# Linear attention with a gated MLP on one core: other positions for the opening, all-VectorE gates and w_in conversions, and x split anew

## The chip, the core and the metric

One core of a Trainium2 chip runs the whole program as one launch. The metric is the device time of an execution in microseconds. A core has TensorE (PE), VectorE (DVE), ScalarE (ACT) and GpSimd (POOL), and SyncE (SP), whose queue here issues all transfers. Each engine works through its own row of instructions in order, and semaphores make one wait for another.

## The reference

An attention with a state of 40x40 for each of 4 batches and 8 heads runs over 768 positions, and its output, 4 x 768 x 320, goes through a gated MLP. Cut to what matters:

```python
for t in range(S):                                   # attention, r k v w a b: (4, 8, 768, 40)
    y[:, :, t] = einsum('bhd,bhde->bhe', rt, state)
    Sa = einsum('bhde,bhe->bhd', state, at)
    state = state * wt[:, :, None, :] - einsum('bhd,bhe->bhde', Sa, bt) \
            + einsum('bhd,bhe->bhde', vt, kt)
x = y.transpose(0, 2, 1, 3).reshape(B, S, H * D)
h = x @ w_in                                         # w_in: (320, 1024)
h = 0.5 * h * (1.0 + tanh(c * (h + 0.044715 * h ** 3)))
u, v = h[..., :512], h[..., 512:]
v_n = (v - mean(v)) / sqrt(var(v) + 1e-06) * g_ln
v_s = einsum('ts,bsd->btd', w_sg, v_n) + b_sg[None, :, None]
return x + (u * v_s) @ w_out                         # w_sg: (768, 768), w_out: (512, 320)
```

## The kernel before

**Attention.** The 768 positions are cut into 12 chunks c of 64, and the 32 heads of all batches into two half-batches f of two batches each. Inside a chunk the recurrence is a triangular system, and between chunks a state `sc` of 40x40 per head is carried.

- *Gates* (`gate_1` to `gate_n`): for each (c, f), VectorE multiplies up the decays (`ex` by scans), makes `at`, and then twice reciprocal, scan (`fixed`) and product: `kb`. TensorE multiplies `ab` from at and kb (16 x 2 products for each half of kb), and transposes kb into `kt`. ACT copies `kbt<-kt` and writes ab's strictly lower blocks as `nts`; VectorE masks what is left of ab back into the tile `at`. `n` is nts transposed by 32x32 blocks.
- *Substitution* (`inv_load`, `inv_in`, `inv_sub`, `inv_end`, `inv_turn`): POOL inverts the triangular blocks of a group of chunks by 29 steps of two operations, `tg<-x,n` and `x<-x,tg`. The groups are (0), (1), (2, 3), (4, 5), (6, 7), (8, 9), (10, 11). VectorE writes n ahead of it and finishes x behind it, then transposes it: `x1z`, `xt`.
- *Back step and chain*: `gp`, `gs`, `xp` turn the inverses into `xt` of a chunk (`post_x`). Then `ru`, `rhsb`, `us`, `vu`, `ut`, `vut`, `pq`, `sp`, `yp` and `yt` follow for each f, and yt goes to `xd`, a copy of x in DRAM.

**MLP.** All products run on a pair of numbers, a high part (h) and a low part (l), both of a short type, in three matmuls. `split64` makes such parts of a stored weight in six steps: the load, ACT's scaled field, VectorE's integer `fields`, ACT's rounding (`wvh`, `wuh`), and `low`, three subtractions on VectorE or POOL. Parts of the MLP run beside the attention as soon as 128 positions of a batch are in xd: `fill_x`, `fill_split`, `fill_low`, `fill_v` and `fill_out` make five of six tiles of v for each batch (`hf`, `hv`), and keep hv in `hd` in DRAM. Here the split halves `xfh` and `xfl` of x go to `xhd` and `xld` in DRAM, too, and `split_x` reads them back in the dense part. For batch 0, `in_v` turns a tile v (two `p` steps on ACT, v on VectorE, then `vh` on ACT and `vl` on POOL) while the last chunk runs. What is left for the end is the dense part: `sg` (w_sg, as `wsh` and `wsl`, by the parts of v), `hf` for u, `gx`, and the output products `op`.

**Order.** No scheduler decides. Each step is registered with a position, and `in_order` sorts all of them; then they are written into the program in that order, so that two steps on one engine stand as their positions do:

```python
y, n = YG[c], GATE[f]
at_(y + n[0], gate_1, c, f, 0)
...
z, v = YI[GROUPS.index(g)], INV if len(g) > 1 else INV1
at_(z + v[0], inv_load, g)
```

`YG` places the gates, `YC` the chains and back steps, `YI` the groups, `DEC` the weight conversions with the steps of `DSTEP` and `DSTEPF` (the first four), `PF` the in_v of batch 0, `BLANKS` POOL's memsets. All engines' calls go through one wrapper, `InOrder.call`, so that every row of the profile has its line, L179; steps are told apart by their tiles.

Of the kernel before, what the change touches and what calls it, by code (L numbers as in the profile page):

```python
# [37 lines left out]
WARMS = ((-4.831, 8), (-4.331, 8))  # L38
BLANKS = -21.0
ZEROS = -36.0  # L40
LOADS = -24.0
# [16 lines left out]
INV1 = (-44.0, -29.3, -27.1, 0.429, -2.0, -1.3)  # L58
BACK = (-3.831, -0.954, -1.454, -2.595, -0.449, 1.071, 3.249)
END_GT = 232.184  # L60
END_IW = 279.907
END_RING = 292.105
END_IV = 314.249
# [25 lines left out]
PO = 232.204  # L89
DECO = (277.194, 283.194, 289.194, 295.194, 301.194, 307.194, 313.194, 319.194)  # L90
# [595 lines left out]
class Mlp:  # L686
# [3 lines left out]
    def __init__(self, tc, ps, xd, w_in, w2, g_ln, wst, b_sg, w_out, decays, out):  # L690
# [6 lines left out]
        self.sb, self.done, self.hd, self.xhd, self.xld = None, set(), None, None, None  # L697
# [176 lines left out]
    def split_cols(self, t, h, l):  # L874
        self.A.copy(out=h, in_=t)
        self.V.tensor_tensor(out=l, in0=t[:, 0:2], in1=h[:, 0:2].bitcast(F32), op=ALU.subtract)
        self.V.tensor_tensor(out=h[64:128, 2], in0=t[64:128, 2], in1=h[64:128, 2].bitcast(F32), op=ALU.subtract)

    def split_x(self, b, n):
        e = 128 * LASTF  # L880
        if (b, 0) not in self.done:
            c = slice(384 * n, 384 * n + 384)
        elif n == 0:
            self.Q.dma_start(out=self.xh[:, :, 0:e].bitcast(F32), in_=self.xhd[b, :, :, 0:e])
            self.Q.dma_start(out=self.xl[:, :, 0:e].bitcast(F32), in_=self.xld[b, :, :, 0:e])
            return
        else:
            c = slice(e, S)
        self.split_cols(self.xts[b % 2][:, :, c], self.xh[:, :, c], self.xl[:, :, c])
# [151 lines left out]
    def side(self):  # L1041
# [38 lines left out]
        for k, p in enumerate(PF):  # L1080
# [5 lines left out]
    def run(self, ahead, verdict=None):  # L1086
# [18 lines left out]
        names = [*FIRSTS] if ahead else [*FILLERS, *FIRSTS]  # L1105
# [75 lines left out]
def attention_then_gated_mlp(tc, ins, out):  # L1181
    nc = tc.nc
    a = ins
    with ExitStack() as ctx:
# [74 lines left out]
```

## Time and profile before

| | |
|---|---|
| time, median of 3 runs | 695.72 us (695.24 to 705.01) |
| the profiled execution | 702.58 us |
| its span, first to last instruction | 700.5 us |
| busy: PE, PEld, DVE, ACT, POOL | 558.7, 509.5, 486.9, 336.1, 351.9 us |
| mean granted TensorE clock | 0.864 of full speed |

The rows below are of the profiled execution, with times from the start of its span. An engine's busy share is a mean over an opening, twelve chunks and a dense part with different limits, so that rows are read by stretch.

### The profile page before, as it was taken

What the parts mean: (1) busy time and instruction counts of PE and PEld (TensorE: products, weight loads), DVE (VectorE), ACT (ScalarE), POOL (GpSimd) and SP (SyncE); (2) the same over time, 40 slices, a digit from 0 to 9 for tenths busy, and PEclk for the clock granted to TensorE, in tenths of its full rate; (3) what the DMA queues carried; (4) which work ended last, traced back from release to release, by engine and by line L of the source; (5) the groups of instructions that cost most, each with busy time, mean ns of one, the idle gap of its engine ahead of it and who ended that gap; (6) DMA issues with size and microseconds to landing.
All of it is one profiled execution on the core that took longest, in us unless ns stands there. A gap on an engine that the chain in (4) does not pass through costs nothing.

```text
span 700.5 us, 25303 instructions
## 1 busy us (share of the span) xinstructions
PE 558.7 (80%) x10710; PEld 509.5 (73%) x10710; DVE 486.9 (70%) x950; ACT 336.1 (48%) x736; POOL 351.9 (50%) x596
## 2 busy tenths in 40 slices
PE   4452766835989989798986979679779999899996
PEld 4352765724878878677875768469779998799995
DVE  5673677766656867765868756537568889969942
ACT  3330547424565767566675566625334434434510
POOL 3186842945585487177566843323244333334331
PEclk8556666765789999899998899779899999999999
DMA  5460262333256565765555556655601465232001
GB/s 185 119 167 6 80 151 83 103 92 106 80 152 163 150 173 149 200 155 138 155 149 153 140 159 167 181 176 159 219 30 63 145 222 153 89 132 73 29 23 39
DMA packets 87138, 89.50 MB, mean 128 GB/s; under 512 B 38280, under 2 KB 69000, under 8 KB 85000
## 3 DMA queue, kind: packets, MB, share of 16 engines
q1 hardware_dynamic: 87016, 87.79, 44.3%
q8 instruction: 86, 1.41, 0.9%
q14 instruction: 36, 0.29, 0.1%
HBM read 68.10 MB, written 19.66 MB: 125 GB/s over the span
## 4 chain that ended last, share of the span: by engine, by line
PE 44%; DVE 16%; issue 6%; ACT 4%; POOL 2%; DMA 2%; SPq 1%; POOLq 0%; ACTq 0%; DVEq 0%
PE sg L179 10%; PE hf L179 5%; PE yp L179 5%; PE op L179 3%; PE ru L179 3%; DVE v L179 3%; PE ut L179 3%; PE pq L179 3%; PE sp L179 2%; DVE p L179 2%; PE ab L179 2%; DVE cv L179 2%; PE xp L179 2%; DVE g L179 2%; PE kt L179 2%
## 5 line engine op out<-in xcount | busy, mean ns | idle before, releaser
L179 POOL TENSOR_TENSOR tg<-x,n 128x135 f32<-128x135 f32 (+25 forms) x203 | 104.1, 513 | 79.9 <-issue 30.7
L179 POOL TENSOR_TENSOR x<-x,tg 128x135 f32<-128x135 f32 (+25 forms) x203 | 106.1, 523 | 15.8
L179 PE MATMUL ab<-at,kb 64*64 64x64 f32 x1536 | 42.4, 268 | 56.3 <-DVE fixed L179 22.7
L179 PEld LDWEIGHTS ab<-at,kb 64*64 64x64 f32 x1536 | 36.9, 175 | 61.0 <-issue 31.8
L179 ACT ACTIVATE nts<-ab 32x512 f32<-32x512 f32 x96 | 46.3, 483 | 57.3 <-PE ab L179 54.4
L179 PE MATMUL sg<-wsh,vh 128*128 128x384 f32 x192 | 66.7, 347 | 5.8 <-ACT wsh L179 3.4
L179 PE MATMUL sg<-wsl,vh 128*128 128x384 f32 x192 | 67.1, 350 | 4.0 <-POOL wsl L179 2.9
L179 POOL TENSOR_TENSOR gx<-g,gy 128x384 fp32r<-128x384 f32 x32 | 34.0, 1066 | 71.6 <-ACT gy L179 71.6
L179 PE MATMUL sg<-wsh,vl 128*128 128x384 f32 x192 | 66.7, 347 | 0.9 <-POOL vl L179 0.9
L179 DVE TENSOR_TENSOR at<-ab,mask 64x512 f32<-64x512 f32 x48 | 32.2, 678 | 42.9 <-ACT nts L179 32.7
L179 POOL TENSOR_TENSOR rs<-rs,mhalf 128x1 f32<-128x1 f32 x24 | 14.9, 624 | 76.0 <-DVE rs L179 72.4
L179 ACT CAST gy<-g 128x384 fp32r<-128x384 f32 x32 | 16.4, 514 | 62.2 <-DVE g L179 59.4
L179 PEld LDWEIGHTS sg<-wsh,vh 128*128 128x128 f32 x192 | 37.2, 194 | 7.0 <-ACT wsh L179 4.4
L179 ACT CAST vh<-v 128x512 fp32r<-128x512 f32 x24 | 14.6, 619 | 56.4 <-DVE v L179 56.4
L179 PEld LDWEIGHTS sg<-wsl,vh 128*128 128x128 f32 x192 | 37.1, 193 | 5.8 <-POOL wsl L179 3.5
L179 DVE TENSOR_TENSOR pqs<-pq,mask 128x512 f32<-128x512 f32 x48 | 30.7, 681 | 14.5 <-PE pq L179 14.5
L179 DVE TENSOR_TENSOR yt<-yp,ex 128x256 f32<-128x256 f32 x48 | 18.1, 417 | 31.5 <-PE yp L179 30.2
L179 PEld LDWEIGHTS sg<-wsh,vl 128*128 128x128 f32 x192 | 37.3, 194 | 2.1 <-POOL vl L179 2.0
L179 PE MATMUL kt<-ident,kb 128*128 128x128 f32 x192 | 35.2, 342 | 2.8 <-issue 2.8
L179 PE MATMUL ut<-ident,vu 64*64 64x64 f32 x768 | 32.2, 235 | 6.1 <-ACT vu L179 6.1
L179 PEld LDWEIGHTS ut<-ident,vu 64*64 64x64 f32 x768 | 28.1, 146 | 11.3 <-ACT vu L179 8.7
L179 POOL TENSOR_TENSOR vl<-v,vh 128x512 fp32r<-128x512 f32 x24 | 31.6, 1320 | 8.8 <-ACT vh L179 8.8
(154 smaller groups left out, 1554.8 us busy)
## 6 DMA issues: line engine op xcount, KB each, us to landing
main<-main SPq DMA_DIRECT2D x44, 321.4 KB
hd<-hv SPq DMA_DIRECT2D x20, 256.0 KB
v<-hd SPq DMA_DIRECT2D x20, 256.0 KB
vu<-vs SPq DMA_DIRECT2D x24, 160.0 KB
vs<-vb SPq DMA_DIRECT2D x24, 160.0 KB
rt<-rt SPq DMA_DIRECT2D x48, 80.0 KB
vut<-vt SPq DMA_DIRECT2D x48, 80.0 KB
xd<-yt SPq DMA_DIRECT2D x96, 40.0 KB
```

What stands on the lines that cost most here:

```text
L179: return self.tc.keep_in_program_order(f(*a, **k))
```

## The change

1. The first eight gates (chunks 0 to 3) have their own positions, `GATE0`, 9.2 apart, and all their steps are VectorE's (`GATEE` is empty; before, both kb of the first two gates and one at were POOL's). With these positions the kt transposes of a gate stand ahead of its ab on TensorE.
2. Groups 0, 1 and 2 of the substitution have their own positions, `INV0`; chunks 2 to 11 all stand 5.17 earlier on the scale, and with them all that is placed beside them. POOL's memsets go to its start.
3. The low parts of all six w_in conversions are VectorE's; before, those of every second were POOL's. The positions of the six change, and the first four loads are asked for earlier.
4. `xhd` and `xld` are gone: fills store their halves no more, and `split_x` splits x again for both halves of every batch, the cast on ACT, the rest on POOL (before, VectorE, and for the last 128 positions alone).
5. The in_v of batch 0 stand 5 to 9 later against chunk 11, and split_x of its second half stands behind them.

```diff
+GATE0 = {(0, 0): (-50.0, (0, 0.6, 1.2, 2.0, 2.1, 3.5, 5.0, 6.2, 6.1, 10.6, 7.4)), (0, 1): (-40.8, (0, 0.6, 1.2, 2.0,
...
-YI = (-3.831, 23.669, 81.0, 132.0, 183.0, 234.0, 285.0)
-GATEE = {(0, 0): "VG", (0, 1): "GG"}
+GATEE = {}
...
-INV1 = (-44.0, -29.3, -27.1, 0.429, -2.0, -1.3)
+INV0 = {0: (-38.7, -31.7, -29.5, 0.443, -3.5, -2.8), 1: (-9.4, -2.4, -0.2, 0.443, 25.8, 26.5), 2: (19.9, 26.9, 29.1,
+    0.702, 70.1, 70.8)}
...
-DSTEPF = (-2.5, -0.5, 0.0, 0.7, 1.4, 2.4)
-DEC = (5.0, 15.0, 25.0, 35.0, 45.0, 55.0, 241.194, 247.194, 253.194, 259.194, 265.194, 271.194)
+DSTEPF = (-9.0, -0.5, 0.0, 0.7, 1.4, 2.4)
+DEC = (10.0, 22.0, 34.0, 46.0, 58.0, 70.0, 236.025, 242.025, 248.025, 254.025, 260.025, 266.025)
...
-PXS = 314.459
+PXS = 321.28
...
-PF = (303.0, 308.0, 313.0, 318.0, 323.0)
+PF = (302.831, 308.831, 314.831, 320.831, 326.831)
...
-                y, n = YG[c], GATE[f]
+                y, n = GATE0.get((c, f)) or (YG[c], GATE[f])
...
-            z, v = YI[GROUPS.index(g)], INV if len(g) > 1 else INV1
+            z, v = (0, INV0[g[0]]) if g[0] in INV0 else (YC[g[0]], INV)
...
+    def split_x(self, b, n):
+        c = slice(384 * n, 384 * n + 384)
+        t, h, l = self.xts[b % 2][:, :, c], self.xh[:, :, c], self.xl[:, :, c]
         self.A.copy(out=h, in_=t)
-        self.V.tensor_tensor(out=l, in0=t[:, 0:2], in1=h[:, 0:2].bitcast(F32), op=ALU.subtract)
...
-        elif n == 0:
-            self.Q.dma_start(out=self.xh[:, :, 0:e].bitcast(F32), in_=self.xhd[b, :, :, 0:e])
-            self.Q.dma_start(out=self.xl[:, :, 0:e].bitcast(F32), in_=self.xld[b, :, :, 0:e])
...
+        self.G.tensor_tensor(out=h[64:128, 2], in0=t[64:128, 2], in1=h[64:128, 2].bitcast(F32), op=ALU.subtract)
+        self.G.tensor_tensor(out=l, in0=t[:, 0:2], in1=h[:, 0:2].bitcast(F32), op=ALU.subtract)
...
-        self.Q.dma_start(out=self.xhd[b, :, :, c], in_=h.bitcast(F32))
-        self.Q.dma_start(out=self.xld[b, :, :, c], in_=l.bitcast(F32))
...
-                steps[k] = self.split64(*self.weights_in()[k], HF // 2, self.G if k % 2 and k < 6 else self.V)
+                steps[k] = self.split64(*self.weights_in()[k], HF // 2, self.V)
```

How the new positions move instructions is seen in the rows of three engines. The first place is VectorE in the opening. Before, from the first kb of gate (1, 0) to n of group 0 (main and ex are numbered by tile, ab by bank; gate (1, 0)'s are `main_96`, `ab_332` and `ab_333`):

```order
L179 TENSOR_TENSOR kb<-main_96,fixed_95 128x2x4x64
L179 RECIPROCAL fixed_94<-call 128x4
L179 SCALAR_TENSOR_TENSOR fixed_95<-main_96,fixed_94 128x260
L179 TENSOR_TENSOR kb<-main_96,fixed_95 128x2x4x64
L179 SCALAR_TENSOR_TENSOR ex_131<-main_97,fixed_94 128x260 x2
L179 TENSOR_TENSOR at_140<-ab_332,mask 64x8x64
L179 TENSOR_TENSOR at_140<-ab_333,mask 64x8x64
L179 TENSOR_SCALAR call<-ex_131 128x8
L179 TENSOR_TENSOR at_141<-main_97,ex_131 128x8x64
L179 STREAM_TRANSPOSE n<-nts_103 128x32x32
```

After, from the second kb of gate (0, 0), `kb<-main_94`, to n of group 0:

```order
L185 TENSOR_TENSOR kb<-main_94,fixed_93 128x2x4x64
L185 SCALAR_TENSOR_TENSOR ex_127<-main_95,fixed_92 128x260 x2
L185 TENSOR_SCALAR call<-ex_127 128x8
L185 TENSOR_TENSOR at_137<-main_95,ex_127 128x8x64
L185 TENSOR_TENSOR at_136<-ab_218,mask 64x8x64
L185 TENSOR_TENSOR at_136<-ab_219,mask 64x8x64
L185 RECIPROCAL fixed_92<-call 128x4
L185 SCALAR_TENSOR_TENSOR fixed_93<-main_95,fixed_92 128x260
L185 TENSOR_TENSOR kb<-main_95,fixed_93 128x2x4x64
L185 RECIPROCAL fixed_92<-call 128x4
L185 SCALAR_TENSOR_TENSOR fixed_93<-main_95,fixed_92 128x260
L185 TENSOR_TENSOR kb<-main_95,fixed_93 128x2x4x64
L185 STREAM_TRANSPOSE n<-nts_101 128x32x32
```

The masks of a gate now stand behind the next gate's at and ahead of its kb, and n of group 0 stands one gate earlier, behind gate (0, 1)'s kb. What the fence can't show is TensorE's row, which before is ab, ab, kt, kt for each gate and now kt, kt, ab, ab.

The second place is POOL in group 2's substitution, at the second conversion inside it (`stg` and `wvl` are a w_in conversion's low part). Before:

```order
L179 TENSOR_TENSOR x<-x,tg 128x17x15
L179 TENSOR_TENSOR tg<-x,n 128x252
L179 TENSOR_TENSOR x<-x,tg 128x18x14
L179 TENSOR_TENSOR stg_1958<-stg_1958,stg_1952 128x256
L179 TENSOR_TENSOR stg_1937<-stg_1937,wvh 128x256
L179 TENSOR_TENSOR wvl<-stg_1937,stg_1958 128x256
L179 TENSOR_TENSOR tg<-x,n 128x247
L179 TENSOR_TENSOR x<-x,tg 128x19x13
L179 TENSOR_TENSOR tg<-x,n 128x240
L179 TENSOR_TENSOR x<-x,tg 128x20x12
```

After, from the same substitution step on:

```order
L185 TENSOR_TENSOR tg<-x,n 128x255
L185 TENSOR_TENSOR x<-x,tg 128x17x15
L185 TENSOR_TENSOR tg<-x,n 128x252
L185 TENSOR_TENSOR x<-x,tg 128x18x14
L185 TENSOR_TENSOR tg<-x,n 128x247
L185 TENSOR_TENSOR x<-x,tg 128x19x13
L185 TENSOR_TENSOR tg<-x,n 128x240
L185 TENSOR_TENSOR x<-x,tg 128x20x12
```

The three operations of the conversion are gone from POOL's row; they stand on VectorE, the last ones around group 2's closing x steps.

The third place is ACT in the last chunk (`p`, `p`, `vh` are a round of in_v; `xt<-xp` and `rhsb` belong to the chain). Before, for the first half-batch:

```order
L179 CAST xfh<-xf 128x384
L179 ACTIVATE p<-v 128x512
L179 ACTIVATE p<-p 128x512
L179 CAST vh<-v 128x512
L179 COPY xt_99<-xp 32x16x32 x2
L179 ACTIVATE cv<-cv 128x64
L179 CAST woh<-stg 128x64
L179 COPY s_7863<-tp 104x320
L179 COPY s_7868<-tp 104x320
L179 ACTIVATE vu_126<-us_7870 64x4x40 x2
```

After:

```order
L185 CAST xfh<-xf 128x384
L185 COPY xt_97<-xp 32x16x32 x2
L185 ACTIVATE p<-v 128x512
L185 ACTIVATE p<-p 128x512
L185 ACTIVATE cv<-cv 128x64
L185 CAST woh<-stg 128x64
L185 COPY s_7798<-tp 104x320
```

The vh of the round that stood ahead of `xt<-xp` is gone from there, and the next round begins behind it. For the second half-batch, before:

```order
L179 ACTIVATE p<-v 128x512
L179 ACTIVATE p<-p 128x512
L179 CAST vh<-v 128x512
L179 COPY rhsb_117<-ru 128x320
L179 ACTIVATE vu_127<-us_8032 64x4x40 x2
L179 ACTIVATE vu_127<-us_8033 64x4x40 x2
L179 CAST xfh<-xf 128x384
L179 COPY vut_125<-ut 104x8x64
```

After, where `xh<-xt` is the cast of split_x:

```order
L185 COPY rhsb_115<-ru 128x320
L185 ACTIVATE vu_125<-us_7954 64x4x40 x2
L185 ACTIVATE vu_125<-us_7955 64x4x40 x2
L185 CAST xfh<-xf 128x384
L185 ACTIVATE p<-v 128x512
L185 ACTIVATE p<-p 128x512
L185 CAST vh<-v 128x512
L185 CAST xh<-xt_7788 128x3x384
L185 COPY vut_123<-ut 104x8x64
```

The round that stood ahead of rhsb now stands behind vu, together with the cast, both ahead of the second `vut<-ut`.

## Rows read from the trace of the kernel before

**Rows 1.** Windows of all engines: stretch, busy PE, PEld, DVE, ACT, POOL, PEclk, DMA, GB/s.

```profile
113.10:169.40 56.30, 32.81 (x860) 28.93 (x856) 37.31 (x79) 24.55 (x57) 39.53 (x64) 0.69 0.42 109
18.00:30.00 12.00, 6.86 (x139) 5.88 (x140) 8.15 (x15) 3.70 (x8) 1.77 (x2) 0.50 0.28 67
```

**Rows 2.** The same window, conversions' stg tiles alone: busy DVE, ACT, POOL.

```profile
113.10:169.40 56.30, 7.06 (x18) 3.56 (x9) 4.85 (x6) 0.69 0.42 109
```

**Rows 3.** Timeline of group 2: start, us, engine, operation, in brackets idle before.

```profile
110.83 2.16 DVE L179 STREAM_TRANSPOSE n<-nts 128x1024 f32<-128x1024 f32 x1
...
121.72 0.73 POOL L179 TENSOR_TENSOR stg<-stg,stg 128x256 f32<-128x256 f32 x1 [4.06 <-ACT wvh L179]
...
152.20 0.72 POOL L179 TENSOR_TENSOR stg<-stg,stg 128x256 f32<-128x256 f32 x1 [8.14 <-ACT wvh L179]
...
169.35 0.76 DVE L179 SCALAR_TENSOR_TENSOR x<-x,n 128x30 f32<-128x30 f32 x3 [3.85 <-POOL x L179]
```

**Rows 4.** Timeline of the first ex, and of gate (1, 0) to group 0's n.

```profile
6.07 1.28 DVE L179 TENSOR_TENSOR_SCAN ex<-main,fixed 128x260 f32<-128x260 f32 x2 [1.81 <-DMA main<-first]
...
25.09 0.17 DVE L179 RECIPROCAL fixed<-call 128x4 f32<-128x4 f32 x1
...
27.69 0.69 DVE L179 TENSOR_TENSOR kb<-main,fixed 128x512 f32<-128x512 f32 x1
...
28.43 1.14 PE L179 MATMUL ab<-at,kb 64*64 64x64 f32 x32 [0.33 <-DVE kb L179]
...
29.50 1.97 PE L179 MATMUL kt<-ident,kb 128*128 128x128 f32 x8
...
29.60 1.98 ACT L179 ACTIVATE nts<-ab 32x512 f32<-32x512 f32 x4 [3.78 <-PE ab L179]
...
31.61 0.68 DVE L179 TENSOR_TENSOR at<-ab,mask 64x512 f32<-64x512 f32 x1 [0.32 <-ACT nts L179]
...
32.89 2.07 DVE L179 STREAM_TRANSPOSE n<-nts 128x1024 f32<-128x1024 f32 x1
```

**Rows 5.** Timeline, VectorE's closing x step of group 0.

```profile
64.50 0.69 DVE L179 SCALAR_TENSOR_TENSOR x<-x,n 128x15 f32<-128x15 f32 x3 [11.00 <-POOL x L179]
```

**Rows 6.** Groups of the six w_in conversions (idle before at the end), and one on the timeline.

```profile
L179 DVE TENSOR_SCALAR stg<-stg 128x256 f32<-128x256 f32 x6 | 1.8, 302 | 13.5 <-ACT stg L179 13.5
L179 ACT ACTIVATE stg<-stg 128x256 f32<-128x256 f32 x6 | 2.6, 434 | 16.6 <-DMA stg<-w 14.5 <-DMA stg<-w_in 2.1
...
149.98 0.62 DVE L179 TENSOR_SCALAR stg<-stg 128x256 f32<-128x256 f32 x2 [6.25 <-ACT stg L179]
```

**Rows 7.** Timeline, one size of substitution step twice on POOL.

```profile
127.47 0.55 POOL L179 TENSOR_TENSOR tg<-x,n 128x207 f32<-128x207 f32 x1
...
160.64 1.13 POOL L179 TENSOR_TENSOR tg<-x,n 128x207 f32<-128x207 f32 x1
```

**Rows 8.** Timeline of chunk 11, ACT and the two us of TensorE.

```profile
439.86 0.26 ACT L179 ACTIVATE cv<-stg 128x64 f32<-128x64 f32 x1 [3.50 <-DMA stg<-w_out]
...
440.87 0.63 ACT L179 ACTIVATE p<-v 128x512 f32<-128x512 f32 x1
...
444.04 0.62 ACT L179 CAST vh<-v 128x512 fp32r<-128x512 f32 x1 [2.02 <-DVE v L179]
...
445.19 0.43 PE L179 MATMUL us<-rhsb,xt 64*64 64x40 f32 x2 [5.84 <-ACT xt L179]
...
458.36 1.09 PE L179 MATMUL us<-rhsb,xt 64*64 64x40 f32 x32 [3.80 <-ACT rhsb L179]
```

**Rows 9.** Groups on POOL, the fills' low parts: busy, mean ns, idle before.

```profile
L179 POOL TENSOR_TENSOR xfl<-xf,xfh 128x256 fp32r<-128x256 f32 x20 | 15.2, 758 | 41.3 <-ACT xfh L179 30.2 <-PE pq L179 7.5 <-DMA hd<-hv 3.3
L179 POOL TENSOR_TENSOR xfh<-xf,xfh 64x128 fp32r<-64x128 f32 x20 | 9.3, 466 | 1.6
```

**Rows 10.** Timeline early in the dense part.

```profile
504.08 0.51 ACT L179 CAST xh<-xt 128x384 fp32r<-128x384 f32 x1 [5.49 <-DMA xt<-xd]
...
514.51 0.44 PE L179 MATMUL sg<-wsl,vh 128*128 128x384 f32 x1 [1.53 <-POOL wsl L179]
```

More of the change, by code (lines that the diff above doesn't have):

```diff
@@ L37 @@
 WARM = 14
[L38 to L41, printed above, removed]
+WARMS = ((-2.6, 8), (-2.1, 8))
+BLANKS = -55.0
+ZEROS = -35.0
+LOADS = -12.0
 PER = 25.5
@@ L49 @@
     29.01, 31.005))
-YC = (0, 27.5, 81.0, 106.5, 132.0, 157.5, 183.0, 208.5, 234.0, 259.5, 285.0, 310.5)
-YG = (35.908, 55.908, 81.0, 106.5, 132.0, 157.5, 183.0, 208.5, 234.0, 259.5, 285.0, 310.5)
-YI = (-3.831, 23.669, 81.0, 132.0, 183.0, 234.0, 285.0)
-GATEE = {(0, 0): "VG", (0, 1): "GG"}
+YC = (2.231, 31.531, 75.831, 101.331, 126.831, 152.331, 177.831, 203.331, 228.831, 254.331, 279.831, 305.331)
+YG = (45.508, 65.508, 85.508, 105.508, 126.831, 152.331, 177.831, 203.331, 228.831, 254.331, 279.831, 305.331)
+GATEE = {}
 GROUPS = ((0,), (1,), (2, 3), (4, 5), (6, 7), (8, 9), (10, 11))
@@ L57 @@
 INV = (-61.011, -53.011, -50.811, 0.759, -6.51, -5.143)
-INV1 = (-44.0, -29.3, -27.1, 0.429, -2.0, -1.3)
+INV0 = {0: (-38.7, -31.7, -29.5, 0.443, -3.5, -2.8), 1: (-9.4, -2.4, -0.2, 0.443, 25.8, 26.5), 2: (19.9, 26.9, 29.1,
+    0.702, 70.1, 70.8)}
 BACK = (-3.831, -0.954, -1.454, -2.595, -0.449, 1.071, 3.249)
[L60 to L63, printed above, removed]
+END_GT = 227.015
+END_IW = 274.738
+END_RING = 286.936
+END_IV = 309.08
 CG = 0.7978845608028654
 G1 = 0.044715
-PIN = 232.194
+PIN = 227.025
 DSTEP = ((-8.5, -1.0, 0.0, 0.7, 1.4, 2.4), (-8.5, -1.0, 0.0, 0.7, 1.4, 2.4))
-DSTEPF = (-2.5, -0.5, 0.0, 0.7, 1.4, 2.4)
-DEC = (5.0, 15.0, 25.0, 35.0, 45.0, 55.0, 241.194, 247.194, 253.194, 259.194, 265.194, 271.194)
+DSTEPF = (-9.0, -0.5, 0.0, 0.7, 1.4, 2.4)
+DEC = (10.0, 22.0, 34.0, 46.0, 58.0, 70.0, 236.025, 242.025, 248.025, 254.025, 260.025, 266.025)
 GE = "VV"
@@ L73 @@
 LASTF = 5
-PX = 314.449
-PXS = 314.459
-PV = 292.205
-PS = 338.954
-PL = 331.954
-PF = (303.0, 308.0, 313.0, 318.0, 323.0)
+PX = 309.28
+PXS = 321.28
+PV = 287.036
+PS = 333.785
+PL = 326.785
+PF = (302.831, 308.831, 314.831, 320.831, 326.831)
 PH = 9
 FILLERS = ("v0", "v1", "v2", "v3", "v4")
-FIRSTS = ("u1", "u0", "u2", "u3", "v5", "u4", "u5", "u6", "u7")
+FIRSTS = ("u1", "u0", "v0", "v1", "u2", "v2", "u3", "v3", "v4", "v5", "u4", "u5", "u6", "u7")
 SEQ = ("s1", "s2", "s0", "s3", "s4", "v0", "s5", "v1", "o0", "o1", "o2", "s6", "s7", "v2", "u0", "v3", "u1", "v4",
@@ L88 @@
 SGS = (5, 3, 5, 6, 7, 8, 8, 11, 10, 11, 12, 11)
-PO = 232.204
-DECO = (277.194, 283.194, 289.194, 295.194, 301.194, 307.194, 313.194, 319.194)
+PO = 227.035
+DECO = (272.025, 278.025, 284.025, 290.025, 296.025, 302.025, 308.025, 314.025)
 DSTEPO = (-8.5, -1.0, 0.0, 0.7, 1.4, 2.4)
@@ L696, in __init__ @@
         self.vn, self.us, self.gs, self.xf = {}, {}, {}, {}
-        self.sb, self.done, self.hd, self.xhd, self.xld = None, set(), None, None, None
+        self.sb, self.done, self.hd = None, set(), None
         self.n, self.todo, self.plan = 0, [], None
@@ L872, in load_x @@
             Q.dma_start(out=t[64 * k:64 * k + 64, 2, c], in_=self.xd[b, 256:320, c])
-    def split_cols(self, t, h, l):
+    def split_x(self, b, n):
+        c = slice(384 * n, 384 * n + 384)
+        t, h, l = self.xts[b % 2][:, :, c], self.xh[:, :, c], self.xl[:, :, c]
         self.A.copy(out=h, in_=t)
-        self.V.tensor_tensor(out=l, in0=t[:, 0:2], in1=h[:, 0:2].bitcast(F32), op=ALU.subtract)
[L877 to L882, printed above, removed]
-        elif n == 0:
-            self.Q.dma_start(out=self.xh[:, :, 0:e].bitcast(F32), in_=self.xhd[b, :, :, 0:e])
-            self.Q.dma_start(out=self.xl[:, :, 0:e].bitcast(F32), in_=self.xld[b, :, :, 0:e])
[L886 to L889, printed above, removed]
+        self.G.tensor_tensor(out=h[64:128, 2], in0=t[64:128, 2], in1=h[64:128, 2].bitcast(F32), op=ALU.subtract)
+        self.G.tensor_tensor(out=l, in0=t[:, 0:2], in1=h[:, 0:2].bitcast(F32), op=ALU.subtract)
     def fill_x(self, b, k):
@@ L909, in fill_low @@
         E.tensor_tensor(out=h[64:128, 2], in0=t[64:128, 2], in1=h[64:128, 2].bitcast(F32), op=ALU.subtract)
-        c = slice(128 * k, 128 * k + 128)
-        self.Q.dma_start(out=self.xhd[b, :, :, c], in_=h.bitcast(F32))
-        self.Q.dma_start(out=self.xld[b, :, :, c], in_=l.bitcast(F32))
         self.xf[b, k] = h, l
@@ L1079, in side @@
         at(PS, self.split_x, 0, 1)
-        for k, p in enumerate(PF):
+        for k, p in enumerate(PF[:LASTF]):
             at(p - PH, self.load_h, 0, k)
@@ L1104, in run @@
         self.open_rest()
-        names = [*FIRSTS] if ahead else [*FILLERS, *FIRSTS]
+        names = [x for x in FIRSTS if x not in FILLERS[:LASTF]] if ahead else [*FILLERS, *FIRSTS]
         seq, jobs = [(x, 0) for x in names], [] if ahead else [(XS, lambda: self.split_x(0, 1))]
@@ L1192, in attention_then_gated_mlp @@
         part.hd = dr.tile([B, LASTF, 128, HF], F32, name="hd")
-        part.xhd = dr.tile([B, 128, 3, S], F32, name="xhd")
-        part.xld = dr.tile([B, 128, 2, S], F32, name="xld")
         verdict = attention(tc, a, xd, flag, keep, ps, part)
```

5 rows, old and new, of the table GATE0 are left out of this document.

## The prediction

> **What bounds the kernel now.** I read the slices of the page first. POOL and VectorE are busy by turns at the start, and TensorE fills up only from about 175 us on. So there are three regimes, an opening, a steady middle and a dense tail, and each needs its own view. The change writes other positions for the opening alone and for the last chunk, and shifts everything between by one constant; in the middle the order of every engine stays as it was.
>
> In the opening the table by stretch shows what is late. From the start of group 2's substitution to its last step, 113.1 to 169.4, POOL works 39.5 of 56.3 us, VectorE 37.3, TensorE 32.8 [rows 1]. No engine is full, so the timeline is next: POOL stands still twice in that stretch, 4.06 and 8.14 us, both times in front of the low part of a w_in conversion that waits for ACT's cast [rows 3]. The substitution's own steps queue behind it, and VectorE's closing x step then waits for POOL (3.85 us). The conversions' six POOL operations take another 4.85 us there [rows 2]. Thus 56.3 − 12.2 − 4.9 = 39.1 us are substitution itself.
>
> Before that, a gate is a loop of kb on VectorE, ab on TensorE, nts on ACT and a mask on VectorE. From 18 to 30 us TensorE's granted clock is 0.50 of full speed, the 1.2 GHz level, and VectorE is busy 8.15 of 12 us [rows 1]: the loop is latency.
>
> At the end of the attention, chunk 11, TensorE's us waits 5.84 us for ACT's xt and, for the other half-batch, 3.80 us for rhsb [rows 8]. In both cases ACT had a round of a v tile's p, p and vh ahead of it.
>
> **Part by part. First gates.** The first two gates leave POOL: their kb took POOL operations, now all is VectorE's. Before, n of group 0 started at 32.89, behind gate (1,0)'s masks. After, it stands right behind gate (0,1)'s kb. The first ex starts at 6.07, the recip–scan–kb pair ends about 5.3 later at 11.4 (a pair takes 25.09 to 28.38, 3.3 us [rows 4]). Then comes the price of the new order on TensorE: the eight kt run ahead of ab. From a pair's end to its last mask it was 28.38 to 32.29, 3.9 us, since ab of the first kb had run under the pair. Now it is kt 1.97 + twice ab 1.14 + nts 1.98 + mask 0.68 + hand-offs = 7.1 [rows 4]. So gate (0,1)'s pair ends at 11.4 + 7.1 + 3.3 = 21.8, and its nts 6.2 later: n starts at 28.0, 4.9 earlier. Each later gate among the first eight costs 7.1 + 3.3 = 10.4 in place of about 7.9, +2.6 at this clock.
>
> **Groups 0 and 1.** Group 0 took 29.5 us from n's end (34.96 [rows 4]) to VectorE's x at 64.50 [rows 5], and POOL's blanking fills leave its inside: it ends at 59.6 or before. But n of group 1 has, by the new order, gates and a conversion in front on VectorE, at +2.6 a gate: I get 64.4 against 65.2, where x ended. The gain of group 0 is eaten. From there to n of group 2 I walked VectorE's new order row by row with these durations: 42.4 in place of 45.6, thus 106.8 in place of 110.83 [rows 3], with 4 us either way for half of the 2.6 of the three gates between (102.8 to 110.8).
>
> **Group 2.** Its conversions leave POOL: stalls gone, 39.1 us left. VectorE gets them. Of 18 conversion operations in the stretch at 7.06/18 = 0.39 us [rows 2] the order makes 26: 10.2 us. So 37.3 − 7.1 + 10.2 = 40.4. Then come VectorE's waits for ACT, since a conversion goes from ACT's scaled field to VectorE and back: 13.5 us over all six, 6.25 of them at 149.98 [rows 6]. ACT itself waited 16.6 for the loads there [rows 6], and a load now stands 9 in place of 2.5 ahead, so I count 2 to 5 in this stretch and take 44 in all: VectorE takes POOL's place as the bound. Closing x step: 106.8 + 2.2 (n) + 44 = 153.0 against 169.35, 16 earlier. Three conversion operations now stand between x and x1z and three more ahead of the next masks and n: 6 × 0.39 = 2.3, say −3 with a hand-off. **Opening: 13 us, ends 6 and 20**; the unchanged middle carries that on, since there every chunk starts from the one before it.
>
> A row speaks against moving work to VectorE: while POOL substitutes, the same tg of 207 elements takes 0.55 us at 127.47 and 1.13 at 160.64 [rows 7]. *By the rule:* the Trainium skill, GPSIMD Engine Reference, section 8 Key points, says that GpSimd shares its SBUF interfaces with VectorE, with contention when VectorE runs an instruction in a 2-port perf mode or with two SBUF inputs, which the two lengths of that row agree with. Nine added two-input operations, at half a microsecond each, would then lengthen POOL's 39.1 to some 43.6, still under VectorE's 44, so that the sum stands.
>
> **Stores of split halves.** The two stores per fill are gone. SP issues every transfer in order, and these two had to wait there for ACT's and POOL's halves. What that cost others I see in one place, POOL's xfl, 3.3 us behind the hd store [rows 9]. **+1, ends 0 and 3.**
>
> **Chunk 11.** The p rounds go behind xt and rhsb. The first wait, 5.84, keeps the part that comes from cv's DMA (3.50 before 439.86 [rows 8]); the round's own time, 440.87 to 444.66 with VectorE's v in it, is 3.8 and goes. Of the second, 3.80, nearly all goes. Added: one round and an xh cast of three times the old columns (3 × 0.51 = 1.5 [rows 10]) now stand ahead of the second vut, 5.3 us, of which TensorE can fill perhaps half with a fill's matmuls. 3.8 + 3.6 − 2.6 = 4.8, **+5, ends 0 and 7**. At the ends the vut side eats both, or is wholly hidden.
>
> **Dense tail.** x is split anew for each half of each batch. ACT casts 1152 columns for each half, where one cast of 384 did for a batch. POOL gets xl and xh: at the fills' rate per element 3 × 0.758 + 3 × 0.466 = 3.7 us per half [rows 9], 29 us over eight halves, where two loads and two short VectorE steps did before. For later batches ten or so microseconds of TensorE's work lie over each. For the first, the split competes with wsl, which POOL also makes and TensorE already waits for (1.53 us at 514.51), and with the cast that waited 5.49 for the load of x at 504.08 [rows 10]. **−2, ends −5 and 0.**
>
> Sum: 13 + 1 + 5 − 2 = 17. The profiled execution took 702.58 (span 700.5 and 2.08 around it): 685.6. It lies 6.86 above the median of the runs, 695.72, and nothing in the sum depends on that offset: 695.7 − 17 = **679**. All good ends together give 20 + 3 + 7 − 0 = 30, thus 666; all bad ones 6 + 0 + 0 − 5 = 1, thus 695. A measurement of this kernel tells about 2%, 13.9 us, from no change.
>
> **The rivals.** *POOL stays the bound of group 2*, since VectorE's gates hide in the waits for ACT: then n of group 2 starts at 105.3 (1.5 before my value, as its row too has such waits), POOL 39.1 behind its 2.2, x at 146.6, 23 earlier than before, less the 3. The opening gives 20 and the time is about 671. For it speaks that VectorE stood still 19 us of the stretch [rows 1]; against it, that these stillnesses are waits for ACT's nts in the gates, which kt ahead of ab makes longer.
>
> *The gates eat it.* If eight gates each cost 2.6 more and all of that is on the path to n of group 2, that is 21 us against the 12.2 + 4.9 freed on POOL and the 4.9 won at n of group 0: a gain of about 1 in the opening, and with the other terms 3 to 5 in all: 690 to 693. For it: the clock of 0.50 and VectorE waiting for nts. Against: gates of chunks 2 and 3 overlap substitution that was the later one, and the clock in the stretch of group 2 is 0.69 [rows 1].
>
> *Loads that hold VectorE, the slower side.* Six conversions stand in VectorE's in-order row, each with a first step that waits for ACT's scaled field, which waits for its load. One such wait was 6.25 us, at 149.98; behind it now stand group 2's last x, x1z and the next gates. At 3.4 us per conversion ((17 + 3.5 counted)/6) the gain is gone, at 5.7 ((17 + 13.9 + 3.5)/6) the kernel is 2% slower, and at 6.25 for all, 37.5 less 3.5, the time is 713. For it: POOL, which could take such a wait before, no longer does. Against: the six waits sum to 13.5, so 2.25 each, and the earlier load shortens them.
>
> *It doesn't do what it says:* the p rounds behind xt leave v late, the dense tail starts as late as before: without chunk 11's 5 us the time is 684, inside the range.
>
> **How the numbers follow.** The forecast (VectorE bounds group 2, 672 to 688) gets 0.52; POOL as the bound (about 671) 0.15; gates eat it (690 to 694) 0.22; the loads 0.08, its whole chance counted as slower, with what else could go wrong; 0.03 for something better than all. The range 666 to 694 holds the first three with little left out on either side. Faster by over 2% is a time under 681.8: some 0.31 of the forecast's 0.52, all of the 0.15 and the 0.03, thus 0.49; slower 0.08; within 2% the rest, 0.43.
>
> **What would show it.** Right: no POOL wait for wvh inside group 2; its x on VectorE at about 153 and waiting little for POOL; n of group 0 near 28; the first gp of chunk 2 some 13 earlier, and the same lead still there at chunk 10; us of chunk 11 without 5.84 and 3.80. Wrong in size: n of group 2 after 111 or the lead gone by the middle, which would mean another thing than the opening sets the pace there, a load or the dense fills. Wrong in sign: stg rows on VectorE with waits of 2 us and more for ACT, between the last tg and x1z above all. In the tail, xl on POOL ahead of the first wsl, with TensorE's wait at that wsl grown from 1.53 to 5.

## The result and the profile after

The changed kernel took 675.82 us (median of 4 runs, 667.34 to 679.25) against 696.64 for the kernel before in the same rounds; the ratio of the undisturbed runs is 0.9597, with a 95% interval of 0.9478 to 0.9716. Two of the four runs lie over 1.5% above the fastest and are left out of the ratio, which therefore stands for 28 us where the medians are 20.8 apart. In a second set of rounds the kernel took 673.53 (6 runs) against 700.92: 0.9587 (0.9530 to 0.9644). The forecast was 679, faster. Its profiled execution took 673.29 us with a span of 671.3.

First the table by stretch of the changed kernel: group 2's substitution from n's end to the closing x, all engines, and then the conversions' stg tiles alone (VectorE, ACT, POOL).

```profile
102.05:147.95 45.90, 31.95 (x880) 29.01 (x884) 42.06 (x89) 24.75 (x56) 34.43 (x58) 0.76 0.45 110
...
102.05:147.95 45.90, 11.80 (x26) 4.04 (x10) 0.00 (x0) 0.76 0.45 110
```

The stretch is 45.9 us for 56.3 [rows 1]. POOL has no conversion in it and works 34.4 us; VectorE is busy 42.1 of 45.9, 26 conversion steps at 0.45 us among it. POOL's last step, in the next fence, ends at 141.08, 6.8 us ahead of the closing x, which waits for nothing: VectorE has become the bound.

The timeline of the changed kernel: VectorE's n of groups 0 to 2, x of groups 0 and 2, POOL's last step of group 2, the transpose behind x, and TensorE's first gp of chunk 2.

```profile
25.18 2.09 DVE L185 STREAM_TRANSPOSE n<-nts 128x1024 f32<-128x1024 f32 x1 [5.20 <-ACT nts L185]
...
54.51 0.68 DVE L185 SCALAR_TENSOR_TENSOR x<-x,n 128x15 f32<-128x15 f32 x3 [2.51 <-POOL x L185]
...
58.63 2.11 DVE L185 STREAM_TRANSPOSE n<-nts 128x1024 f32<-128x1024 f32 x1
...
99.95 2.10 DVE L185 STREAM_TRANSPOSE n<-nts 128x1024 f32<-128x1024 f32 x1
...
140.64 0.44 POOL L185 TENSOR_TENSOR x<-x,tg 128x87 f32<-128x87 f32 x1
...
147.91 0.76 DVE L185 SCALAR_TENSOR_TENSOR x<-x,n 128x30 f32<-128x30 f32 x3
...
149.44 1.94 DVE L185 STREAM_TRANSPOSE x1z<-x 128x1024 f32<-128x1024 f32 x1
...
151.53 1.92 PE L185 MATMUL gp<-x1z,nts 64*32 64x32 f32 x64 [0.98 <-DVE x1z L185]
```

Against [rows 3 to 5], n of group 0 is 7.7 earlier, n of group 2 10.9, its x 21.4; x does not wait for POOL any more (3.85 before). The first gp of chunk 2 stood at 172.19 in the kernel before, so the opening gives 20.7 us:

```profile
172.19 0.45 PE L179 MATMUL gp<-x1z,nts 64*32 64x32 f32 x9 [3.79 <-DVE x1z L179]
```

The first gate shows what the new order costs. Timeline of the changed kernel, gate (0, 0) from its second kb to its last mask:

```profile
10.38 0.69 DVE L185 TENSOR_TENSOR kb<-main,fixed 128x512 f32<-128x512 f32 x1
...
11.12 1.12 PE L185 MATMUL kt<-ident,kb 128*128 128x128 f32 x4 [0.38 <-DVE kb L185]
...
12.17 1.99 PE L185 MATMUL ab<-at,kb 64*64 64x64 f32 x64
...
14.19 0.98 ACT L185 ACTIVATE nts<-ab 32x512 f32<-32x512 f32 x2 [1.49 <-PE ab L185]
...
16.20 0.68 DVE L185 TENSOR_TENSOR at<-ab,mask 64x512 f32<-64x512 f32 x1 [0.26 <-ACT nts L185]
```

Only four kt stand behind the second kb, since the other four ran under the second pair, and the 64 ab take 1.99 in a row. From kb's end to the mask's end it is 5.8 us, not 7.1.

Last the three later stretches, as windows: the middle (gp of chunk 2 to gp of chunk 11), the last chunk to the last yp, and the dense part to just behind its last computing instruction (the span runs on for another 4.6 us before and 5.9 after); busy PE, PEld, DVE, ACT, POOL, clock, DMA, GB/s. The kernel before:

```profile
172.20:430.90 258.70, 225.56 (x6706) 200.36 (x6708) 183.59 (x352) 162.71 (x366) 161.26 (x282) 0.92 0.57 150
430.90:473.00 42.10, 29.85 (x730) 25.12 (x729) 21.05 (x51) 20.05 (x47) 12.59 (x22) 0.76 0.60 177
473.00:695.90 222.90, 208.86 (x1132) 199.06 (x1130) 168.96 (x325) 85.09 (x173) 79.91 (x79) 0.98 0.33 107
```

The changed kernel:

```profile
151.50:401.40 249.90, 223.00 (x6704) 199.15 (x6704) 186.32 (x361) 162.78 (x367) 162.18 (x282) 0.92 0.52 136
401.40:436.20 34.80, 28.32 (x730) 23.82 (x729) 18.73 (x45) 22.65 (x50) 17.18 (x25) 0.75 0.49 135
436.20:665.40 229.20, 211.85 (x1130) 201.29 (x1130) 168.17 (x317) 89.44 (x175) 100.69 (x93) 0.96 0.26 81
```

The middle gives 8.8, the last chunk 7.3, the dense part takes 6.3 back, and 1.3 go behind it; with the opening that is the 29.2 us by which the spans differ. All four places moved by more than I had put down for them.

### The profile page after: what moved, and what is told of

Its sections match the earlier page's. It is cut to its first block, busy times and chain, and to the rows that moved or that the text cites. A ratio compares the mean times of both kernels' runs of the same rounds, so it can differ in the third digit from the quotient of the medians.

```text
span 671.3 us, 25229 instructions
## 1 busy us (share of the span) xinstructions
PE 557.3 (83%) x10710; PEld 507.4 (76%) x10710; DVE 492.3 (73%) x956; ACT 342.4 (51%) x740; POOL 365.0 (54%) x598
## 4 chain that ended last, share of the span: by engine, by line
PE 45%; DVE 26%; issue 9%; POOL 8%; ACT 6%; DMA 4%; SPq 1%; POOLq 0%; DVEq 0%; ACTq 0%
PE yp L185 6%; PE hf L185 5%; PE sg L185 5%; PE ut L185 4%; PE ru L185 3%; PE ab L185 3%; PE sp L185 3%; DVE v L185 3%; PE pq L185 3%; PE xp L185 3%; DVE g L185 2%; DVE p L185 2%; PE kt L185 2%; PE op L185 2%; DVE stg L185 2%
## 5 line engine op out<-in xcount | busy, mean ns | idle before, releaser
L185 POOL TENSOR_TENSOR tg<-x,n 128x135 f32<-128x135 f32 (+25 forms) x203 | 106.4, 524 | 102.3 <-DVE n L185 63.0
L185 PEld LDWEIGHTS kt<-ident,kb 128*128 128x128 f32 x192 | 26.3, 168 | 37.5 <-issue 26.9
L185 POOL TENSOR_TENSOR rs<-rs,mhalf 128x1 f32<-128x1 f32 x24 | 14.9, 624 | 65.3 <-DVE rs L185 61.6
L185 PE MATMUL ab<-at,kb 64*64 64x64 f32 x1536 | 40.3, 269 | 9.8 <-DVE fixed L185 7.4
L185 PEld LDWEIGHTS ut<-ident,vu 64*64 64x64 f32 x768 | 29.2, 150 | 12.2 <-ACT vu L185 6.7
L185 DVE SCALAR_TENSOR_TENSOR g<-sg,gl,bt 128x384 f32<-128x384 f32 x32 | 19.6, 611 | 24.7 <-PE sg L185 13.6
```

The lines of the kernel that those rows point to most:

```text
L185: return self.tc.keep_in_program_order(f(*a, **k))
```

## The experiments

Each time is the median of 6 runs, each ratio is against the kernel before on the same chip, with its 95% interval. The first four shared a chip (before: 702.0), the next four another (700.92), the last four a third (699.07). Executions of one kernel scatter by 5 us and more either way; so I read places in the trace first. Places scatter too: six traces share the changed kernel's opening (the changed kernel twice, stores back, old in_v, opening alone, stores late), and their first gp of chunk 2 lies between 148.79 and 155.06. A shift of a few us there counts only with a row that names it.

**Which engine makes the low parts.** In the changed kernel:

```diff
-                steps[k] = self.split64(*self.weights_in()[k], HF // 2, self.V)
+                steps[k] = self.split64(*self.weights_in()[k], HF // 2, self.G if k % 2 and k < 6 else self.V)
```

> The changed kernel, but with the low parts of every second w_in conversion back on GpSimd. Theory A (the conversions' waits on GpSimd were what made group 2 long): two GpSimd rows that wait for wvh stand in group 2 again, the time from n of group 2 to its closing x on VectorE grows from 48 towards the 58.5 of before, and the kernel is 6 to 12 us slower than the changed one. Rival B (VectorE is the bound of group 2 now, and GpSimd has 11 us of slack there): group 2 stays at 45 to 50 us, the kernel within 3 us of the changed one.

677.87 us, 0.9715 (0.9651 to 0.9778); gp of chunk 2 at 152.41. Timeline of this kernel, POOL's conversions in groups 1 and 2 and VectorE's closing x of group 2:

```profile
94.97 0.72 POOL L185 TENSOR_TENSOR stg<-stg,stg 128x256 f32<-128x256 f32 x1 [7.74 <-ACT stg L185]
...
125.39 0.72 POOL L185 TENSOR_TENSOR stg<-stg,stg 128x256 f32<-128x256 f32 x1 [5.44 <-ACT stg L185]
...
148.78 0.77 DVE L185 SCALAR_TENSOR_TENSOR x<-x,n 128x30 f32<-128x30 f32 x3 [0.32 <-POOL x L185]
```

Rival B holds in the trace: in group 2 POOL stands still 5.44 us again, less than the 8.14 and 4.06 of [rows 3] together, x waits only 0.32 for POOL and comes 0.9 later, inside the scatter. In group 1 POOL stands still 7.74, but with one pair of substitution steps left, and x comes at 97.81 for 97.79. With the new places and the early loads, the engine of the low parts is not what shortened group 2. The ratio lies above the changed kernel's, on another chip; what this trace loses it loses behind gp of chunk 11, where both kernels have the same code.

**Stores of the halves, and rounds of in_v.** Three kernels: the changed one with `xhd` and `xld` stored and read back as before; the changed one with the old places of in_v; and both of these with the old place of split_x, so that only opening and conversions are new.

```diff
+        self.Q.dma_start(out=self.xhd[b, :, :, c], in_=h.bitcast(F32))
+        self.Q.dma_start(out=self.xld[b, :, :, c], in_=l.bitcast(F32))
```

> The changed kernel with the stores of the split halves of x and the loads in the dense part as before. Theory A: the 9 us that the changed kernel gains between chunk 2 and chunk 10 come from the stores that are gone; the lead of chunk 10 over the kernel before falls from 30 to about 21, the dense part gains back 4 to 7 us, so that the kernel is 2 to 5 us slower than the changed one. Rival B: the 9 us are no work of the stores but a difference of the two executions; the middle keeps its pace, the dense part gains 4 to 7, and the kernel is 4 to 7 us faster than the changed one.

```diff
-PF = (302.831, 308.831, 314.831, 320.831, 326.831)
+PF = (297.831, 302.831, 307.831, 312.831, 317.831)
```

> The changed kernel with the in_v rounds of batch 0 at their old places against the last chunk. Theory A: us waits for xt and rhsb again, 5.8 and 3.8 us, and the last yp comes 6 to 8 us later, so does the end. Rival B: the rounds cost the chain as much where they stand now (ahead of vut, where pq waits 2.8 us) or are given back behind the attention, since the v tiles are needed at the start of the dense part anyway: within 3 us of the changed kernel.

> The new opening with all conversions on VectorE, and nothing else: stores and loads of the split halves, in_v rounds and split_x stand as before. Theory A: the lead at the first gp of chunk 2 is 20 us as in the changed kernel and stays 20 to the end: 17 to 21 us faster than the kernel before. Rival B (the middle gains by itself from the new opening, or the execution of before was a long one): the lead grows to 28 in the middle, and the kernel is 25 to 30 us faster than the one before.

They took 684.21 (0.9751, 0.9685 to 0.9817), 680.27 (0.9712, 0.9640 to 0.9784) and 680.91 (0.9725, 0.9671 to 0.9779). The first line of the windows of each, the middle, with the stores (stores back; opening alone) and without (old in_v):

```profile
155.10:411.30 256.20, 225.12 (x6705) 198.73 (x6705) 185.83 (x359) 162.88 (x367) 162.39 (x282) 0.92 0.57 152
```

```profile
148.80:405.10 256.30, 227.02 (x6704) 201.35 (x6704) 183.66 (x352) 163.16 (x368) 160.85 (x282) 0.91 0.57 152
```

```profile
151.80:403.70 251.90, 227.86 (x6706) 203.23 (x6708) 187.75 (x360) 162.90 (x368) 163.66 (x282) 0.90 0.52 135
```

Over all kernels here the middle takes 253.4 to 258.7 us with the stores at their old place (four traces, mean 256.2) and 246.5 to 253.4 without (nine, mean 250.3). The stores cost about 6 us there, with the two ranges just meeting at 253.4, as theory A of the first of the three had it. Its other half failed: with the loads back the dense part stays at 229.2, and with the old in_v it is 231.3; only with both old is it 225.1. The last chunk takes 41.3 with both old and 37.2, 37.1 and 34.8 with the new in_v alone, without stores alone and with both. From gp of chunk 11 to the end the sums are 266.4 (opening alone), 266.4 (stores back), 268.3 (old in_v) and 264.0 (changed): what chunk 11 gains is taken back behind it, and a second kernel with the changed one's code there, that of the first experiment, took 270.0. Over all traces in_v, split and loads come to nothing there: from gp of chunk 11 to the last matmul it is 264.1 to 265.4 in the three with the old code and 261.6 to 269.0, mean 264.5, in the eight with the changed kernel's. With the old in_v places the wait for rhsb is back in full (3.79), that for xt only with 1.98. Opening alone lies 19.3 us under the kernel before by its ratio, its theory A.

**The changed kernel again**, beside the next three.

> The changed kernel once more, on the chip and in the rounds of the three beside it. If the executions scatter by some us, as the runs so far do, its time lies 18 to 28 us below the kernel before; the way from gp of chunk 2 to gp of chunk 11 is 246 to 252 us as in the three kernels without the stores, not 256 to 259 as in the three with them.

673.53, 0.9587; gp at 151.64 and 401.95, the middle 250.3. As expected.

**Conversions without positions, and positions without conversions.** The kernel before with the new `DEC`, `DSTEPF` and VectorE for all low parts; and the changed one with the old three.

```diff
-DSTEPF = (-2.5, -0.5, 0.0, 0.7, 1.4, 2.4)
-DEC = (5.0, 15.0, 25.0, 35.0, 45.0, 55.0, 241.194, 247.194, 253.194, 259.194, 265.194, 271.194)
+DSTEPF = (-9.0, -0.5, 0.0, 0.7, 1.4, 2.4)
+DEC = (10.0, 22.0, 34.0, 46.0, 58.0, 70.0, 241.194, 247.194, 253.194, 259.194, 265.194, 271.194)
```

> The kernel before, with the w_in conversions of the changed one: low parts on VectorE, their positions and the earlier loads. Theory A (the conversions' waits on GpSimd inside group 2 held the opening): first gp of chunk 2 comes 8 to 14 us earlier than 172, the whole kernel 8 to 14 us faster than before. Rival B (the positions of gates and groups set the opening, as the trial with two engines for the low parts suggests): 0 to 5 us.

> The changed kernel with the w_in conversions as before: their old positions, late loads, and every second low part on GpSimd. Theory A: waits for wvh stand in GpSimd's group 2 or in VectorE's row for ACT's stg, group 2 lengthens by 6 to 12 us, first gp of chunk 2 at 157 to 164. Rival B (positions of gates and groups alone give the opening): gp within 3 us of 151.5.

690.54 (0.9846, 0.9803 to 0.9890), gp at 160.27: 11.9 earlier, theory A. And 691.42 (0.9856, 0.9811 to 0.9901), gp at 171.19: 19.7 later than in the changed kernel, more than expected. Timeline of the second: VectorE's and ACT's steps of conversions, POOL's stalls and last step, and x in group 1, then POOL's stalls in group 2:

```profile
72.99 1.02 DVE L185 TENSOR_SCALAR stg<-stg 128x256 f32<-128x256 f32 x2 [8.57 <-ACT stg L185]
...
90.39 0.43 ACT L185 ACTIVATE stg<-stg 128x256 f32<-128x256 f32 x1 [2.59 <-DMA stg<-w_in]
...
90.86 0.62 DVE L185 TENSOR_SCALAR stg<-stg 128x256 f32<-128x256 f32 x2 [6.95 <-ACT stg L185]
...
93.32 0.72 POOL L185 TENSOR_TENSOR stg<-stg,stg 128x256 f32<-128x256 f32 x1 [13.72 <-ACT stg L185]
...
102.92 0.27 POOL L185 TENSOR_TENSOR x<-x,tg 128x45 f32<-128x45 f32 x1
...
111.66 0.68 DVE L185 SCALAR_TENSOR_TENSOR x<-x,n 128x15 f32<-128x15 f32 x3
...
129.53 1.12 POOL L185 TENSOR_TENSOR stg<-stg,stg 128x256 f32<-128x256 f32 x1 [7.40 <-ACT wvh L185]
...
155.78 0.73 POOL L185 TENSOR_TENSOR stg<-stg,stg 128x256 f32<-128x256 f32 x1 [2.48 <-ACT wvh L185]
```

The stalls are back, in group 1 with 13.72 for 3.75 in the kernel before. But POOL isn't what holds group 1: its last step ends at 103.19, and x comes only at 111.66, against 97.79 in the changed kernel. VectorE's own row is late. It stands still 8.57, 6.95 and 3.73 us at the first steps of three conversions, for ACT's field step, which itself waits for the load; in the changed kernel all its waits at conversion steps up to that x are 6.1 us. So 13.9 of the 19.7 us are there at x of group 1, and loads that hold VectorE brought them. With conversions as before, the new positions alone give the opening 1 us (171.19 for 172.19); with the new ones they give 8.7 (160.27 to 151.53). The two parts of the change alone give 12.9 of the 20.7, and the rest only together.

**Loads alone.** The changed kernel with `DSTEPF` beginning at -2.5. These steps hold for all six w_in conversions (`k < 6` in the kernel), not for the first four alone.

> The changed kernel, but with the six w_in loads asked for 2.5 ahead of their conversion as before, in place of 9. Theory A (the stalls of the opening were the conversions waiting for late loads, whichever engine does the low part): ACT's stg waits for the DMA again, VectorE for ACT 2 to 4 us at each of the six conversions, the first gp of chunk 2 comes 8 to 18 us after 151.5, the kernel 8 to 18 us slower than the changed one. Rival B (the places of the conversions between the gates did it): gp within 3 us of 151.5.

683.36 (0.9825, 0.9754 to 0.9896), gp at 156.41. Timeline of this kernel, ACT's field step of conversions 5 and 6:

```profile
139.33 0.45 ACT L185 ACTIVATE stg<-stg 128x256 f32<-128x256 f32 x1 [5.83 <-DMA stg<-w_in]
...
151.80 0.43 ACT L185 ACTIVATE stg<-stg 128x256 f32<-128x256 f32 x1 [4.77 <-DMA stg<-w]
```

Theory A in kind, but not in size: 4.9 us and two waits for the DMA, not six; VectorE waits 2.65 and 2.77 behind them. The earlier four conversions waited for no load. So of the 19.7 us the engine alone is worth 1 and late loads alone 5. Late loads at the old places are worth 13.9 by x of group 1; how much of that is the place and how much the load isn't shown, since no run changed the places alone.

**kt ahead of ab.** The changed kernel with ab ahead of kt; and then with nts ahead of kbt on ACT as well, the old order in full. Each of the eight entries of `GATE0` changes alike; the first:

```diff
-(0, 0.6, 1.2, 2.0, 2.1, 3.5, 5.0, 6.2, 6.1, 10.6, 7.4)
+(0, 0.6, 1.2, 2.0, 2.1, 3.5, 5.0, 6.2, 4.9, 10.6, 7.4)
```

The second:

```diff
-(0, 0.6, 1.2, 2.0, 2.1, 3.5, 5.0, 6.2, 6.1, 10.6, 7.4)
+(0, 0.6, 1.2, 2.0, 2.1, 3.5, 5.0, 7.4, 4.9, 10.6, 6.2)
```

> The changed kernel with ab ahead of kt again in the first eight gates. Theory A (each gate's loop has about 1 us in it for kt, some 8 us for eight gates, of which those before n of group 2 are on the path): n of group 2 starts 2 to 6 us earlier than 99.95, the first gp of chunk 2 as much. Rival B (n of group 2 waits for the end of group 1's substitution, not for gates): n and gp within 1.5 us.

680.97 (0.9731, 0.9684 to 0.9778); n of group 2 at 102.84, gp at 155.13: later, not earlier. On ACT kbt, which now waits for the later kt, stood in front of nts, so that nts began at 14.51 in place of 14.19. In the second kernel nts stands in front again.

> The changed kernel with the old order inside the first eight gates in full: ab ahead of kt on TensorE and nts ahead of kbt on ACT. Theory A (kt first costs each gate about 1 us, and the trial before lost time only because kbt stood ahead of nts): n of group 0 at about 24, n of group 2 at 95 to 98, first gp of chunk 2 2 to 5 us earlier than 151.5. Rival B (TensorE's lower clock between 60 and 100 us, 0.64 for 0.76 in that trial, came with ab first and eats it): gp at 151 to 155.

667.74 us, 0.9587 (0.9522 to 0.9651), with n of group 2 at 94.70. Timeline of this kernel, gate (0, 0) as above, then n of group 0 and the first gp of chunk 2:

```profile
11.15 0.94 PE L185 MATMUL ab<-at,kb 64*64 64x64 f32 x32 [0.86 <-DVE kb L185]
...
12.11 1.98 ACT L185 ACTIVATE nts<-ab 32x512 f32<-32x512 f32 x4 [3.47 <-PE ab L185]
...
14.12 0.68 DVE L185 TENSOR_TENSOR at<-ab,mask 64x512 f32<-64x512 f32 x1 [0.26 <-ACT nts L185]
...
21.20 2.10 DVE L185 STREAM_TRANSPOSE n<-nts 128x1024 f32<-128x1024 f32 x1 [3.22 <-ACT nts L185]
...
146.47 1.20 PE L185 MATMUL gp<-x1z,nts 64*32 64x32 f32 x64 [1.38 <-DVE x1z L185]
```

The last mask starts 2.1 us earlier than in the changed kernel, n of group 0 4.0 earlier after two gates, gp 5.1: theory A. The clock from 60 to 100 us is 0.71, for 0.64 in the kernel just above and 0.76 in the changed one. Its median is the lowest of all. Against the changed kernel the trace shows 5 us in the opening; the ratios of the two (0.9587 both) don't tell them apart.

**What the stores cost by.** The stores and loads kept, but each pair asked for behind the hd store.

> The changed kernel with the stores and loads of the split halves, but each pair of stores asked for behind the hd store of its fill, when its data has long been there. Theory A (the 6 us of the middle were SyncE's queue standing in order behind the two waits): gp of chunk 2 to gp of chunk 11 takes 247 to 252 us as without stores. Rival B (it was the traffic of the stores): 255 to 258 us as with them at the old place.

684.84 (0.9852, 0.9773 to 0.9930); the middle 254.4. That is within the range with the stores at their old place and 1.0 above the highest without, and neither theory's range has it. Whether queue or traffic is the cause stays open.

**The last conversion behind x1z.** `DEC`'s sixth from 70.0 to 74.0 in the changed kernel.

> The changed kernel with the sixth w_in conversion 4 later, behind group 2's closing x and its two transposes. Theory A (its VectorE steps around x and x1z lie on the path): x1z starts 0.8 to 2 us earlier behind x, gp of chunk 2 at 149 to 151, the kernel 1 to 3 us faster than the changed one. Rival B (the conversion then delays the first fill of chunk 2 or the next gates by as much): within 1 us of it.

678.60 (0.9742, 0.9672 to 0.9812). x1z starts 0.79 behind x in place of 1.53, but x itself is at 148.60 and gp at 151.54, the same as in the changed kernel: rival B, as far as one trace can tell. What is won behind x is lost ahead of it.

## Why the prediction was right, and which terms were not

The total, 17 us forecast against 20.8 to 27.4 in the medians, 28 by the ratio and 29.3 between the two profiled executions, lies in the range, and so does the time. That the first median is only 3 us from 679 is luck: the places add up to 12 us more than the forecast, since two terms were too small, and two others nearly cancel.

*Opening, 13 forecast, 20.7 measured, just past its upper end of 20.* Its mechanism held: no POOL wait in group 2, VectorE as the bound with 42.1 of 45.9 us, n to x 48.0 for my 46.2. What was mis-sized is n of group 2, 99.95 for 106.8; n of group 1 was already at 58.63 for my 64.4, so that the gain of group 0 was not eaten. I had charged each gate a loop of 10.4 us; from the end of the first gate's second kb (11.07) to that of the next (19.99) it is 8.9, since half of kt hides under the second pair and ab runs in one piece. That kt first costs a gate something was right: 2.0 us each by the last gate experiment, for my 2.6. The six conversion steps behind x cost 0.8 between x and gp where I took 3. Two of my differences are a tenth off (56.3 − 12.2 − 4.9 is 39.2, and 10.4 − 7.9 is 2.5); nothing hangs on it.

*Cause of the stalls.* I let them go because the low parts leave POOL. The runs put 1 us on that, about 5 on the earlier loads alone, and most of the rest on loads and places together, by VectorE's row. The row of the stall names POOL and ACT's wvh; the wait behind it was one for a load and for a turn in VectorE's row. In the kernel before, POOL's stall of 8.14 begins at 144.06, and the conversion's first step on ACT stands 5.5 us later:

```profile
149.52 0.43 ACT L179 ACTIVATE stg<-stg 128x256 f32<-128x256 f32 x1 [6.36 <-DMA stg<-w]
```

*Stores, 1 forecast (0 to 3), about 6 measured.* In proportion this is the term that was furthest off, and the step of the working that failed. I priced the two stores by the one POOL wait at which I saw somebody else waiting, 3.3 us; the middle as a whole is 6 us shorter without them, and which wait that is stays open.

*Chunk 11, 5 forecast (0 to 7), 7.3 measured;* both us waits of [rows 8] are gone, and pq waits for vut instead, by the changed kernel's timeline on TensorE:

```profile
409.23 0.63 PE L185 MATMUL us<-rhsb,xt 64*64 64x40 f32 x32
...
417.30 1.97 PE L185 MATMUL pq<-rt,vut 40*64 40x64 f32 x60 [2.78 <-ACT vut L185]
...
419.13 1.06 PE L185 MATMUL us<-rhsb,xt 64*64 64x40 f32 x29
```

*Dense part, −2 forecast (−5 to 0), −6.3 measured:* TensorE is busy 3.0 us longer there at a clock of 0.96 for 0.98 and idle 3.3 longer. Counted by TensorE's matmuls behind the last yp, the changed kernel is 3.0 us behind the kernel before at the 189th of 1129 and 6.3 at the last. The later 3.3 are the new split of x, which I had hidden under ten us of TensorE's work: from the 189th on the nine traces with it take 3.2 to 4.4 us more than the kernel before, and the four others with the old split −1.0 to 0.5. With only the stores and loads put back that part falls away, but the start takes 6.1 in place of 3.0. The sign that I named isn't there: the wait for wsl is 1.34 for 1.53. Forecast as independent, chunk 11 and the dense part belong together: from the first gp of chunk 11 to the end of the last window it is 265.0 before and 264.0 after.

*The rivals.* POOL as the bound fell: its last step ends 6.8 us ahead of x. That its opening of 20 came nearer than my 13 does not speak for it. "The gates eat it" fell: kt first costs 2.0 a gate, but gp of chunk 2 only 5.1, where the rival had 21. Chunk 11 without its gain came true in the number, but not by the v that comes late: the first sg starts 14.9 us behind the last yp in both kernels, and the loss comes after it. Loads that hold VectorE: in the changed kernel no first step on ACT waits for a load. With late loads at the old places they do hold it, 8.57 and 6.95 us. With late loads at the new places the two long waits are ACT's, 5.83 and 4.77, VectorE waits 2.65 and 2.77 behind them, under the 3.4 per conversion at which the gain would be gone. The rule on GpSimd's shared SBUF interfaces (the Trainium skill, GPSIMD Engine Reference, section 8 Key points) left the forecast as it was, and its price does not show: with VectorE busy 42.1 of 45.9 us in place of 37.3 of 56.3, POOL's busy time on the substitution of group 2 is 34.4 us, and was 39.5 − 4.9 = 34.7 before.

## What to carry to other kernels

When an engine stands still in front of a piece of another chain, follow that chain to its load before you blame the engine that shows the wait: here putting the work back on the other engine cost 1 us, and putting its places and loads back as well 19.7. Price a transfer that is taken away by the stretch it runs in and not only by the waits that name it. And where an early step gains at the end of one stage, add the next stage to the window: 7.3 us of the last chunk came back as 6.3 in the dense part.

## What was not expected of the hardware

At the start of the dense part TensorE stands still twice close together, before the change for 1.45 and 1.53 us at 511.1 and 513.0, in the changed kernel for 1.62 and 1.34 us at 474.9 and 477.2. In the changed kernel the granted clock falls to 0.66 in the 6 us from 479.4, between its two levels of 1.2 and 2.4 GHz, while before it stayed at 1.00, the upper one. The lengths of the gaps don't decide that: in all other traces it falls there too, to 0.59 to 0.77, also in the four whose gaps are within 0.01 of those (0.72, 0.77, 0.63 and 0.62). Part of what the changed kernel loses in the first 49 us of the dense part goes with a fall of the clock that the one trace of before did not have: the traces of opening alone and of conversions alone, with the old code there and the fall, are already 1.7 and 1.9 us behind it at the 189th matmul, and the changed kernel 3.0.
